# Chunk-selected attention with a gated convolution block: the selection masks of the later pairs transposed by DMA instead of TensorE

## The chip, the core and the metric

The kernel runs on one core of a Trainium2 chip. A core has five engines, each with its own queue of instructions that it works through in order: TensorE (PE; the loading of its weights is listed apart as PEld), VectorE (DVE), ScalarE (ACT), GpSimd (POOL) and SyncE (SP), which here does nothing but issue DMAs. Engines wait for each other by semaphores only. The metric is the device time of one execution in microseconds: 198.59 us before the change (median of 3 runs, 198.16 to 199.49). The profiled execution has a span of 195.8 us.

## The reference

There are 4 batches, 8 heads, 768 positions and a head dimension of 64, all in float32. The keys are cut into 24 chunks of 32. For each query, an upper bound of its score with each chunk is computed from the chunk's elementwise minimum and maximum; the 6 chunks with the highest bounds, among those that are not in the future, are kept, and ordinary causal attention runs on these alone:

```python
k_min = np.min(k_chunks, axis=3)
k_max = np.max(k_chunks, axis=3)
ub = np.sum(np.maximum(q[:, :, :, None, :] * k_min[:, :, None, :, :],
                       q[:, :, :, None, :] * k_max[:, :, None, :, :]), axis=-1)
ub = np.where(causal, ub, -1000000000.0)
top_chunks = np.argsort(ub, axis=-1)[..., -top_k:]
scores = scale * np.matmul(q, k.transpose(0, 1, 3, 2))
sel = (j_chunk == top_chunks[..., None]).any(axis=-2)
mask = sel & (pos[:, None] >= pos[None, :])
scores = np.where(mask, scores, -1000000000.0)
```

The attention output x, 768 x 512 per batch, then goes through a gated block: a causal convolution over 5 positions per channel gives the gate, `x @ w_val` the value, and the result is `(sigmoid(conv(x)) * (x @ w_val)) @ w_out`.

## The kernel before, in words

**Pairs.** Two heads of one batch make a pair; there are 16 pairs, numbered 0 to 15, four per batch. A pair passes through these stages:

- `load`: k, q and v of both heads come by DMA (192 KB for one head), three pairs ahead of their use.
- `kq`: TensorE transposes k and q in float32 (L561). ScalarE copies them out of PSUM (L576, L622, L634), VectorE takes the minima and maxima of chunks (L581), GpSimd writes the operands KE and QU of the score matmul in float16 (L606, L653).
- `sel` and `part`, the selection, on which the change bears. For each of the five blocks of 128 queries after the first, two float32 matmuls (L727) give the bounds of both heads. VectorE adds a term for the query's own chunks (L740), finds the sixth highest bound with ten MAX8 instructions (L746), and one comparison (L753) writes `NS`, a 128 x 5 x 128 tile that says for each query which chunks are not selected. The score matmul wants this with chunks on the partitions. So TensorE transposes the five blocks into a PSUM bank (L764), and two copies (L787) of 24 partitions x 640, one on VectorE for head 0 and one on ScalarE for head 1, bring the rows into `QU`.
- `attn`: the score matmuls (L860) contract over 64 rows of q and k and, in the same pass, over the 24 mask rows, against constant rows that are -240 where a key lies in that chunk: a chunk that isn't selected gets a large negative score. There are 28 such matmuls for a pair, in 11 PSUM banks. ScalarE takes the exponential of each bank (L867), GpSimd zeroes the future part of diagonal blocks (L874), 42 matmuls multiply by v (L891), VectorE divides by the sums (L817, L821), and a DMA transpose (`to_xT`, L833) puts the result in the layout that the gated block wants.
- `moe_gate`, `moe_val`, `moe_out`: the gate of a pair's 128 channels is one convolution tap on TensorE (L932), four on VectorE (L956) and a tanh on ScalarE (L961). After every fourth pair, a batch's values (L975), products (L982) and outputs (L991, L997) follow, and stores to HBM (L1004).

**The order of the work** is not written by hand. The code registers every operation with an engine, a cost, a key (a due time in units of pairs), what it reads and writes, and which buffers it takes. `Plan.order` then starts operations one after the other on a model of the engines: on each engine the one with the lowest key among those that could start about earliest. The table `SHIFT` moves the keys by kind of operation ("DVE:QM" for the mask copies on VectorE, "PE:s" for the scores; a leading 0 is for the first pair), and `CAPS` says how many of the eight PSUM banks each use may hold. The outcome is one list, and each engine's queue is its part of that list. DMAs are operations of SyncE. When one has been started, the model does this:

```python
            elif e in ("SP", "ACTQ"):
                free[e] = s + 0.55
                dma = max(dma, s + 1.6) + o.cost
                o.end = dma + 0.8
            ...
            for d in o.outs:
                if d.eng != e:
                    d.ready = max(d.ready, o.end)
                elif e != "PE":
                    d.ready = max(d.ready, free[e] + 0.06)
```

**Buffers.** QU and KE have three copies each, used in turn by pair, so mask rows of pair p can only be written when the scores of pair p - 3 are done. NS has two copies. A switch `MDMA` stood at 99, which no pair reaches; the branch that it guards was unused.

Of the kernel before, what the change touches and what calls it, by code (L numbers as in the profile page):

```python
# [10 lines left out]
F16 = mybir.dt.float16  # L11
# [293 lines left out]
def kernel(  # L305
# [10 lines left out]
    nc = tc.nc  # L316

    B, H, S, D = q.shape
# [12 lines left out]
    CP = (slice(64, 64 + NCH), slice(0, NCH))  # L331
# [4 lines left out]
    SEL0 = 128  # L336
    SELT = NT - 1
# [5 lines left out]
    X0 = XP - (KSZ - 1)  # L343
    MASKS = ("DVE", "ACT")

    MDMA = 99
    KBPOOL = True

    SHUF = 99
# [8 lines left out]


    SHIFT = {  # L360
        "0SP:kn": -1.6, "0SP:qn": -1.1, "0SP:cwn": 3.4, "0DVE:warmup": 3.35, "0POOL:E00": -5.1,
        "0POOL:cfill": -4.5, "0DVE:KB": 0.9, "0DVE:QM": 2.7, "0POOL:VA": -3.3, "PE:pcw": 1.4,
        "0DVE:kmx": -3.1, "0DVE:kmn": -2.3, "0ACT:KE": -1.9, "0DVE:kmrr": 1.1, "0PE:qnT": 1.4,
        "0ACT:rq": 2.5, "SP:qn": -1.3, "PE:pu": 2.5, "DVE:top8": 1.8, "PE:sT": 0.1,
        "DVE:QM": 1.8, "ACT:QM": -3.0, "PE:knT": -0.92, "ACT:k32": -1.3, "DVE:kmx": 1.0,
        "DVE:kmn": 1.5, "POOL:kmrr": -0.7, "POOL:KBh": -7.4, "PE:qnT": -0.87, "ACT:q32": -1.6,
        "ACT:rq": -1.1, "POOL:QU": 1.5, "POOL:VA": 1.2, "PE:s": 0.14, "bank0": 1.1, "ACT:P": 1.9,
        "POOL:Ptri": -1.6, "PE:av": -4.2, "bank1": 0.34, "bank2": -3.5, "0PE:av": 3.77,
        "DVE:rcp": 2.0, "DVE:onat": -4.0, "bank3": 1.0, "bank4": -0.6, "bank5": 1.3,
        "bank6": 0.5, "bank7": -1.9, "bank8": 0.2, "bank9": 0.72, "bank10": 0.9, "PE:pg": 2.1,  # L370
        "PE:pv": 2.66, "DVE:gv": -2.9, "PE:po": 2.5, "ACT:osb": 2.3,
    }
    CAPS = {"w": 5, "s": 4, "av": 2, "spare": 1, "v": 4}
    BUFS = {"kn": 3, "qn": 3, "vn": 3, "P5": 2, "kmx": 2, "kmr": 2,
# [14 lines left out]
    junk = cpool.tile([128, 512], F16, tag="junk")  # L389
    warmup = cpool.tile([128, 1], FP, tag="warmup")  # L390
    cfill = cpool.tile([128, SELT, 2, 4], FP, tag="cfill")
# [19 lines left out]
    T = {}  # L411
# [22 lines left out]
    def act(key, cost, fn, r=(), w=(), new=()):  # L434
        plan.add("ACT", key, cost, fn, r, w, new)
# [7 lines left out]
    def sp(key, kb, fn, r=(), w=(), new=(), eng="SP", rate=205.0, at=0.0):  # L443
        plan.add(eng, key, kb / rate, fn, r, w, new, at=at)
# [263 lines left out]
    def part(p, key, g, its, nch, kb, qu, ns, iN, i2):  # L708
        pu, n, i0 = ("pu", p, g), len(its), its[0] - 1
        i1 = i0 + n  # L710

        def cols(t):

            x = "p (s c) -> p s c" if len(t.shape) == 2 else "p i (s c) -> p i s c"
            y = t.rearrange(x, s=2)
            return y[:, :, 0:nch] if len(t.shape) == 2 else y[:, :, :, 0:nch]

        first = new(pu, "w", [128, n * (2 * NCH + 4) + 4 * its[0]])
        kbr = [("KBh", i2, hh, w) for hh in range(2) for w in range(nch // 12)]

        def bound(i):
            return T[pu][:, i * 2 * NCH:(i + 1) * 2 * NCH]

        for it in its:
            ts = slice(it * 128, (it + 1) * 128)
            for j, x in enumerate(("rq", "q32")):
                pe(key, 128, lambda it=it, ts=ts, j=j, x=x: nc.tensor.matmul(  # L727
                    out=cols(bound(it - 1 - i0)), lhsT=T[x, p][:, ts],
                    rhs=cols(kb[:, j, :]), start=(j == 0), stop=(j == 1)),
                    r=[(x, p), (x, p, it // 3)] + kbr,  # L730
                    w=((pu, it),), new=first if it == its[0] and j == 0 else (), kind="u")
                plan.also((pu,))

        def own():

            x, d = 2 * NCH + 4, 4 * its[0]
            t = T[pu][:, d:d + n * x].rearrange("p (i x) -> p i x", i=n)
            return t[:, :, 0:2 * NCH].rearrange("p i (s c) -> p i s c", s=2)[:, :, :, 0:4]

        dve(key, 0.12, lambda: nc.vector.tensor_tensor(  # L740
            out=own(), in0=own(), in1=cfill[:, i0:i1], op=ALU.add),
            r=[pu, "cfill"] + [(pu, it) for it in its], w=((pu, "own"),))
        for it in its:
            m = 4 * it + 4
            for s in range(2):
                dve(key + 0.1, 0.08, lambda it=it, s=s, m=m: nc.vector.max(  # L746
                    out=T["top8", p][:, it - 1, s, :],
                    in_=bound(it - 1 - i0)[:, s * NCH:s * NCH + m]),
                    r=(pu, (pu, it), (pu, "own")), w=(("top8", p, it, s),),
                    new=new(("top8", p), "top8", [128, SELT, 2, 8])  # L750
                    if it == 1 and s == 0 else ())
                plan.also((("top8", p),))
        dve(key + 0.2, 0.07 + n * nch * 2 / 960, lambda: nc.vector.tensor_tensor(  # L753
            out=ns.rearrange("p i (s c) -> p i s c", s=2)[:, i0:i1, :, 0:nch],
            in0=cols(T[pu][:, 0:n * 2 * NCH].rearrange("p (i c) -> p i c", i=n)),
            in1=T["top8", p][:, i0:i1, :, 5:6].to_broadcast([128, n, 2, nch]), op=ALU.is_lt),
            r=[pu, (pu, "own"), ("top8", p)] + [(pu, it) for it in its]
            + [("top8", p, it, s) for it in its for s in range(2)]
            + ([("NS", i2, 1 - g)] if len(its) < SELT else []),
            w=[("NS", i2, g)] if len(its) < SELT else [("NS", i2, 0), ("NS", i2, 1)])  # L760
        pt = ("sT", p, g)
        q0, nq = its[0] * 128, n * 128
        for i in range(n):
            pe(key + 0.3, 128, lambda i=i: nc.tensor.transpose(  # L764
                out=T[pt][:, i * 128:(i + 1) * 128], in_=ns[:, i0 + i, :], identity=identh),
                r=(("NS", i2, g), "identh"), w=((pt, i),),
                new=new(pt, "w", [128, nq], F16) if i == 0 else (), kind="x")
            plan.also((pt,))

        def mask(key, hh, fn, r, w):  # L770
            if MASKS[hh] == "ACT":
                act(key, 0.2 + nq * 0.0006, lambda: fn(copy=nc.scalar.copy), r, w)
            else:
                dve(key, 0.14 + nq * 0.00057, lambda: fn(copy=nc.vector.tensor_copy), r, w)

        ws = (g,) if len(its) < SELT else (0, 1)
        if p >= MDMA:
            act(key + 0.35, 0.14 + nq * 0.0007, lambda: nc.scalar.copy(out=T["m16", p], in_=T[pt]),
                r=[pt] + [(pt, i) for i in range(n)], w=(("m16", p),),
                new=new(("m16", p), "m16", [128, S - SEL0], F16))  # L780
            for hh in range(2):
                sp(key + 0.35, 60, lambda hh=hh: nc.sync.dma_start(
                    out=qu[CP[hh], hh, SEL0:S], in_=T["m16", p][CP[hh], :]),
                    r=(("m16", p),), w=[("QM", iN, hh, w) for w in ws])
            return
        for hh in range(2):
            mask(key + 0.35, hh, lambda hh=hh, copy=None: copy(  # L787
                out=qu[CP[hh], hh, q0:q0 + nq],
                in_=T[pt][CP[hh], :]),
                r=[pt] + [(pt, i) for i in range(n)], w=[("QM", iN, hh, w) for w in ws])  # L790
# [14 lines left out]
    def attn(p, key):  # L805
# [24 lines left out]
        def to_xT(ws, kk):  # L830
            t0, n = 3 * ws[0], 3 * len(ws)
            if p < NPAIR - 1:
                sp(kk, n * 32, lambda: nc.sync.dma_start_transpose(  # L833
                    out=xT[:, slot, XP + t0 * 128:XP + (t0 + n) * 128]
                    .rearrange("p (t r) -> p t r", t=n),
                    in_=T["onat", p][:, t0:t0 + n, :].rearrange("p t d -> p (t d)")),
                    r=[("onat", p)] + [("onat", p, w) for w in ws],
                    w=[("xT", slot, w) for w in ws], rate=200.0)
                return
            pt = ("xTp", p, ws[0])  # L840
            for i in range(n):
                pe(kk, 128, lambda i=i: nc.tensor.transpose(
                    out=T[pt][:, i * 128:(i + 1) * 128], in_=T["onat", p][:, t0 + i, :],
                    identity=identh),
                    r=(("onat", p), ("onat", p, (t0 + i) // 3), "identh", pt), w=((pt, i),),
                    new=new(pt, "w", [128, n * 128], F16) if i == 0 else (), kind="x")
            act(kk, 0.11 + n * 0.0915, lambda: nc.scalar.copy(
                out=xT[:, slot, XP + t0 * 128:XP + (t0 + n) * 128], in_=T[pt]),
                r=[pt] + [(pt, i) for i in range(n)], w=[("xT", slot, w) for w in ws])
# [266 lines left out]
```

## Time and profile before

| what | value |
|---|---|
| time, median of 3 runs | 198.59 us |
| span of the profiled execution | 195.8 us |
| DMA traffic | 29.56 MB, mean 151 GB/s |
| transposes of the masks, TensorE (L764) | 80 instructions |
| copies of the masks (L787) | 17 on ScalarE, 17 on VectorE |
| DMAs with transposes (L833) | 15, landing after a median of 3.6 us |

When a pair's mask was made and used (us from the start, read from the trace):

| pair | bounds done | NS done | first transpose | copies done (ACT, DVE) | first score |
|---|---|---|---|---|---|
| 8 | 80.8 | 89.3 | 89.4 | 90.7, 91.5 | 90.9 |
| 9 | 90.5 | 98.8 | 99.0 | 100.2, 102.1 | 100.6 |
| 11 | 111.0 | 114.9 | 116.0 | 117.2, 119.2 | 119.5 |
| 13 | 133.1 | 136.5 | 136.5 | 137.8, 140.2 | 140.2 |
| 15 | 152.9 | 155.3 | 156.2 | 157.3, 158.4 | 158.5 |

In the groups of the profile a line reads: source line, engine, operation, what is written and read, how many; then the sum of their busy times and the mean length of one in ns; then how long the engine had been idle just before them and what ended most of that. "SPq" is SyncE's queue. The chain of work that ended last is followed back from the last instruction, at each step to what released it. A TensorE record includes the time in the array, so neighbouring records overlap.

### The profile page before, as it was taken

The numbers are of one execution on the slowest core, as the hardware profiler recorded it, in microseconds if no ns is written. First come the engines' busy times: TensorE is split into PE (matmuls) and PEld (weight loads), VectorE is DVE, ScalarE is ACT, GpSimd is POOL, SyncE is SP. The second block draws the span as 40 slices with busy tenths as digits, with TensorE's granted clock in tenths as the row PEclk, the third lists the DMA queues.
The fourth block names the chain that finished last, engine by engine and source line by source line (L and its number), as shares of the span: only waits on it lengthen the run. The fifth ranks groups of instructions, "written<-read, shape, count | busy, mean of one in ns | idle before, by whom it ended". The sixth has DMA issues, their size and how long they took to land.

```text
span 195.8 us, 5815 instructions
## 1 busy us (share of the span) xinstructions
PE 181.2 (93%) x2043; PEld 144.2 (74%) x2043; DVE 177.5 (91%) x540; ACT 162.1 (83%) x355; POOL 122.9 (63%) x274
## 2 busy tenths in 40 slices
PE   6598989999589999999999999999999999999981
PEld 2377878989568988888887878797979657765530
DVE  7839599979889999899999999999999999999981
ACT  3688969999969999997979999998897999945431
POOL 8029779889767998889894856886788334200000
PEclk9889999999999999999999999999999999999999
DMA  6999999999999999997997664242005430305244
GB/s 135 223 217 216 211 223 180 151 229 212 188 228 221 190 179 181 183 177 163 146 181 180 172 148 139 87 90 44 2 5 147 122 136 7 75 3 216 111 162 161
DMA packets 91900, 29.56 MB, mean 151 GB/s; under 512 B 87754, under 2 KB 88798, under 8 KB 91870
## 3 DMA queue, kind: packets, MB, share of 16 engines
q1 hardware_dynamic: 89214, 27.74, 70.1%
q0 software_dynamic: 1056, 1.05, 3.8%
q10 hardware_dynamic: 1600, 0.39, 1.0%
q8 instruction: 16, 0.26, 0.6%
q14 instruction: 14, 0.11, 0.2%
HBM read 20.98 MB, written 6.29 MB: 139 GB/s over the span
## 4 chain that ended last, share of the span: by engine, by line
PE 63%; DVE 16%; ACT 9%; DMA 5%; issue 2%; POOL 2%; SPq 1%; ACTq 0%; POOLq 0%
PE banks L860 13%; PE banks L727 11%; PE banks L975 9%; PE banks L991 9%; PE banks L891 8%; PE banks L561 7%; DVE banks L956 6%; ACT t_P L867 5%; PE banks L932 4%; DMA t_kn<-in_k_dram 3%; DMA xT<-t_onat 2%; PE banks L764 2%; DVE t_kmx L581 2%; DVE t_kmr L581 1%; PE banks L543 1%
## 5 line engine op out<-in xcount | busy, mean ns | idle before, releaser
L867 ACT ACTIVATE t_P<-banks 128x512 f16<-128x512 f32 (+1 forms) x176 | 91.4, 599 | 4.4 <-PE banks L860 4.2
L956 DVE SCALAR_TENSOR_TENSOR banks<-xT,cwT,banks 128x384 f32<-128x384 f16 x128 | 77.1, 619 | 2.7 <-PE banks L932 1.9
L860 PE MATMUL banks<-QU,KE 128*128 128x128 f16 (+4 forms) x448 | 65.6, 246 | 1.6 <-DVE QU L787 0.7
L874 POOL TENSOR_SCALAR_AFFINE_SELECT t_P<-t_P 128x384 f16<-128x384 f16 x64 | 32.8, 522 | 24.9 <-ACT t_P L867 23.8
L860 PEld LDWEIGHTS <-KE 128*128 128x128 f16 (+1 forms) x448 | 39.3, 108 | 8.3 <-DVE QU L787 1.3
L606 POOL CAST KE<-t_k 64x384 f16<-64x384 f32 x60 | 30.0, 504 | 13.8 <-ACT t_k L576 9.4
L653 POOL CAST QU<-t_q 64x384 f16<-64x384 f32 x60 | 30.3, 504 | 3.1 <-ACT t_q L622 0.7
L891 PE MATMUL banks<-VA,t_P 128*128 128x65 f16 x672 | 29.8, 194 | 0.6 <-ACT t_rq L634 0.4
L891 PEld LDWEIGHTS <-t_P 128*128 128x128 f16 x672 | 26.3, 98 | 5.1 <-POOL t_P L874 1.4
L975 PE MATMUL banks<-xT,wval_sb 128*128 128x384 f16 x128 | 29.6, 325 | 0.1
L727 PE MATMUL banks<-KB,t_rq 128*128 128x48 f32 (+1 forms) x160 | 27.9, 256 | 0.0
L727 PE MATMUL banks<-KB,t_q 128*128 128x48 f32 (+1 forms) x160 | 27.6, 254 | 0.0
L727 PEld LDWEIGHTS banks<-KB,t_rq 128*128 128x128 f32 x160 | 26.1, 191 | 1.5 <-DVE t_onat L821 0.7
L727 PEld LDWEIGHTS banks<-KB,t_q 128*128 128x128 f32 x160 | 26.2, 191 | 0.3
L991 PE MATMUL banks<-wout_sb,t_gv 128*128 128x512 f16 x96 | 25.8, 379 | 0.6 <-DVE t_gv L982 0.6
L961 ACT ACTIVATE t_g<-banks 128x384 f32<-128x384 f32 x32 | 16.0, 500 | 5.8 <-DVE banks L956 5.7
L561 PE MATMUL banks<-ident,t_kn 128*128 128x128 f32 x96 | 17.3, 286 | 2.6 <-DMA t_kn<-in_k_dram 2.3
L932 PE MATMUL banks<-xT,diag 128*128 128x384 f16 x64 | 17.4, 326 | 2.3 <-DMA xT<-t_onat 2.0
L622 ACT ACTIVATE t_q<-banks 128x384 f32<-128x384 f32 x32 | 16.0, 501 | 3.7 <-PE banks L561 3.6
L576 ACT ACTIVATE t_k<-banks 128x384 f32<-128x384 f32 x32 | 16.3, 512 | 2.9 <-PE banks L561 2.6
L997 ACT ACTIVATE t_osb<-banks 128x512 f32<-128x512 f32 x22 | 13.2, 600 | 6.3 <-PE banks L991 4.2
L821 DVE TENSOR_TENSOR t_onat<-banks,t_rcp 128x384 f16<-128x384 f32 x32 | 17.7, 553 | 0.2
(62 smaller groups left out, 264.5 us busy)
## 6 DMA issues: line engine op xcount, KB each, us to landing
t_vn<-in_v_dram SPq DMA_DIRECT2D x32, 192.0 KB, 4.3
out_dram<-t_osb SPq DMA_DIRECT2D x24, 256.0 KB, 2.2
t_kn<-in_k_dram SPq DMA_DIRECT2D x30, 192.0 KB, 4.6
t_qn<-in_q_dram SPq DMA_DIRECT2D x30, 192.0 KB, 3.9
wval_sb<-in_moe_w_val_dram POOLq DMA_DIRECT2D x1, 512.0 KB, 7.3
wout_sb<-in_moe_w_out_dram POOLq DMA_DIRECT2D x1, 512.0 KB, 7.3
xT<-t_onat SPq DMA_TRANSPOSE x15, 3.6
t_kn<-in_k_dram ACTq DMA_DIRECT2D x2, 96.0 KB, 3.1
```

The source lines that it names most:

```text
L561: lambda tl=tl: nc.tensor.transpose(out=T[name][:, tl * 128:(tl + 1) * 128], in_=T[which, p][:, 3 * w + tl, :], identity=ident),
L606: pool(k0 + 0.6, 0.56, lambda hh=hh: nc.gpsimd.tensor_copy(out=ke[HP[hh], hh, sl], in_=T["k32", p][HP[hh], sl]), r=(("k32", p), ("k32", p, ...
L653: pool(k0 + 0.3, 0.56, lambda hh=hh: nc.gpsimd.tensor_copy(out=qu[HP[hh], hh, sl], in_=T["q32", p][HP[hh], sl]), r=(("q32", p, w), ("q32", ...
L727: pe(key, 128, lambda it=it, ts=ts, j=j, x=x: nc.tensor.matmul(out=cols(bound(it - 1 - i0)), lhsT=T[x, p][:, ts], rhs=cols(kb[:, j, :]), s ...
L860: pe(kk, m, lambda hh=hh, c=c, jt=jt, q0=q0, m=m, bank=bank: nc.tensor.matmul(out=T[bank][:, c:c + m], lhsT=ke[KP[hh], hh, jt * 128:(jt + ...
L867: nc.scalar.activation(out=T[pt][:, 0:width], in_=T[bank][:, 0:width], func=AF.Exp, scale=0.125),
L874: nc.gpsimd.affine_select(out=ap, in_=ap, pattern=[[0, tris], [1, 128]], compare_op=ALU.is_ge, fill=0.0, base=0, channel_multiplier=-1)
L891: nc.tensor.matmul(out=T[pav][:, o0:o0 + D + 1], lhsT=T[pt][:, col:col + 128], rhs=va[:, hh, jt, :], start=st, stop=sp_, skip_group_check= ...
L932: nc.tensor.matmul(out=T[pg], lhsT=diag[ct][:, ki, hl, :], rhs=xT[:, slot, X0 + w * HB + ki:X0 + w * HB + ki + HB], start=(n == 0), stop=( ...
L956: nc.vector.scalar_tensor_tensor(out=both() if whole else T[pgs[w]], in0=x_of(X0 + ki, w), scalar=cwT[:, i:i + 1], in1=both() if whole els ...
L975: lambda ct=ct: nc.tensor.matmul(out=T[pv], lhsT=wval_sb[:, ct, et * 128:(et + 1) * 128], rhs=xT[:, slot0 + ct, XP + w * HB:XP + (w + 1) * ...
L991: pe(key, DM, lambda et=et: nc.tensor.matmul(out=T[po], lhsT=T["gv", b, et][:, s * 128:(s + 1) * 128], rhs=wout_sb[:, et, :], start=(et == ...
```

## The change

From pair 8 on the mask takes another road. SyncE issues a DMA that transposes the whole `NS` tile (five blocks of 128 x 128) into a new SBUF tile `m16`, and two DMAs that copy 24 rows of 640 from `m16` into `QU`, one for each head. The TensorE transposes, the PSUM bank and the two copies of these pairs are gone. Pairs 0 to 7 keep the old road. The planner's rate for the DMA transposes of the attention output is set from 200 to 133. `SHIFT` has new values throughout, so the order of all operations is a different one, in the first half too.

```diff
-    MDMA = 99
+    MDMA = 8
...
     SHIFT = {
...
+        q0, nq = its[0] * 128, n * 128
+        if p >= MDMA:
+            sp(key + 0.3, 160, lambda: nc.sync.dma_start_transpose(
+                out=T["m16", p], in_=ns.rearrange("p i c -> p (i c)")),
+                r=(("NS", i2, 0), ("NS", i2, 1)), w=(("m16", p),),
+                new=new(("m16", p), "m16", [128, SELT, 128], F16), rate=133.0)
+            for hh in range(2):
+                sp(key + 0.35, 60, lambda hh=hh: nc.sync.dma_start(
+                    out=qu[CP[hh], hh, 128:S],
+                    in_=T["m16", p][CP[hh]].rearrange("p i c -> p (i c)")),
+                    r=(("m16", p),), w=[("QM", iN, hh, w) for w in range(2)], rate=240.0)
+            return
         pt = ("sT", p, g)
-        q0, nq = its[0] * 128, n * 128
...
         ws = (g,) if len(its) < SELT else (0, 1)
-        if p >= MDMA:
...
-            return
...
-                    w=[("xT", slot, w) for w in ws], rate=200.0)
+                    w=[("xT", slot, w) for w in ws], rate=133.0)
```

## The prediction, made before the result was known

> **What bounds the kernel now.** I read the busy line of the page first, then busy time by stretch from pair 8 on, then TensorE's waits, then the groups that the change removes, then the DMA landings.
>
> ```profile
> PE 181.2 (93%) x2043; PEld 144.2 (74%) x2043; DVE 177.5 (91%) x540; ACT 162.1 (83%) x355; POOL 122.9 (63%) x274
> ...
> PE 63%; DVE 16%; ACT 9%; DMA 5%; issue 2%; POOL 2%; SPq 1%; ACTq 0%; POOLq 0%
> ```
>
> Three engines are nearly full, and the chain that ended last runs mostly through TensorE. Busy time overstates them: records overlap. In the timeline a 128-column score starts 0.056 us after the one before it, though its record is 0.219 us long; a VectorE multiply-add (L956) starts 0.525 us after its neighbour with a record of 0.62. So I count spacings: 0.030 us for a P·V matmul, 0.163 for 384 columns, 0.216 for 512, 0.16 for a bound matmul (L727), 0.109 for a float32 transpose.
>
> ```profile
> 90.00:160.00 70.00, 69.94 (x821) 57.22 (x820) 68.77 (x210) 64.00 (x138) 50.14 (x110) 1.00 0.51 117
> 160.00:172.00 12.00, 11.85 (x182) 8.70 (x178) 12.00 (x28) 11.00 (x24) 3.63 (x7) 1.00 0.24 57
> 172.00:196.00 24.00, 18.98 (x104) 9.23 (x101) 18.48 (x36) 9.44 (x18) 0.00 (x0) 0.99 0.36 132
> ```
>
> Columns: length, then busy time of PE, PEld, DVE, ACT, POOL, then clock, DMA share and GB/s. From 90 to 160 us, where masks 9 to 15 are made, TensorE's spacings sum to 67.3 of 70.0 us; those of VectorE to about 93%, of ScalarE to about 86%. TensorE is the bound, with only 2.7 us of small waits left; VectorE is next. DMA is half idle there, and nearly so after 130 us.
>
> ```profile
> PE banks L764 <- DVE NS L753: 1.3, 2, 0.9
> PE banks L860 <- DVE QU L787: 0.7, 1, 0.7
> ```
>
> These are all of TensorE's long waits for a mask (total, times, longest), and both lie before 30 us. From pair 8 on a mask is never waited for long: its road is short.
>
> **What the Trainium skill says.** "DMA: Bandwidth & Descriptors", Rules for kernel authors: a DMA that reads what an earlier DMA wrote must wait for that one's completion semaphore before it is issued; the same queue doesn't order them. The same page, Anatomy of one DMA: the wait happens on the issuing sequencer, and a fixed part, about 2 us for DMAs issued from GpSimd, is mostly the wait for the last write's receipt. The trace agrees on the size: stores of 256 KB land 2.0 us after issue when nothing else runs. It shows no DMA that waits for another's data. "Perfetto Trace Analysis", Optimizing Scalar/DVE Operations: instruction latency exceeds engine time, since the write acknowledgement overlaps the next instruction. The trace agrees: 0.62 against 0.525 us above.
>
> **What goes.** For eight pairs:
>
> ```profile
> L787 ACT COPY QU<-banks 24x640 f16<-24x640 f16 (+2 forms) x17 | 11.1, 652 | 2.3 <-PE banks L764 2.2
> L787 DVE COPY QU<-banks 24x640 f16<-24x640 f16 (+2 forms) x17 | 8.0, 469 | 1.1 <-ACT QU L787 0.6
> L764 PE MATMUL banks<-identh,NS 128*128 128x128 f16 x80 | 7.6, 220 | 1.3 <-DVE NS L753 1.3
> ```
>
> TensorE: 8 x 5 transposes x 0.056 = 2.24 us, all of it on the bounding engine. VectorE: 8 x 0.52 (spacing of the 640-wide copy) = 4.2 us. ScalarE: 8 x 0.58 = 4.6 us. These two are not the bound; what they bring is fewer of the 2.7 us of waits, and a bank less in use per pair. In the tail, 24 us hold 18.8 us of TensorE spacings and VectorE is full from 172 to 184, so a lighter VectorE can shorten it: I take 1 us (bounds 0 and 2). I cost the memory and DMA traffic at nothing: eight transposes of 160 KB and sixteen small copies go into queues half idle from 100 us on.
>
> **What comes: a longer road.** All DMAs go through SyncE. Its chain is now: wait for NS, issue the transpose, wait until it has landed, issue copy 0, issue copy 1; TensorE's first score of each head waits for its copy.
>
> ```profile
> L833 SPq DMA_TRANSPOSE xT<-t_onat x15: 1212/1222/2605, 30.8 to 169.2; - x15
> ...
> DMA to landing us min/median/max: 2.8/3.6/4.7
> ```
>
> The nearest row, a transpose of six blocks against five here, lands after 2.8 us when the queue is empty (all those after 130 us) and 4.4 when loads are ahead (92 us). The copy of 24 rows of 1280 B is shown nowhere; I bound it by 1.6 and 2.3 us empty (the smallest store landing is 2.0), and take 1.9; under loads 2.7, the least landing of a load near there, with 3.5 as the upper bound. With 0.1 us between, the mask of head 0 comes 2.8 + 0.1 + 1.9 = 4.8 us after the issue (bounds 4.3 and 5.3), under loads 4.4 + 0.1 + 2.7 = 7.2 (5.6 to 8.0). Head 1 follows 0.4 later, more if other issues stand between.
>
> Is that much work ahead of the score in TensorE's order? The order of the changed kernel tells. I counted the matmuls between the transpose and the first score of head 0 and 1, in the single list that the planner writes out, and priced them with the spacings times 70.0/67.3. First a test on the kernel before, from the start of NS to the first score: counted 1.8, 2.0, 2.5, 5.0, 1.8, 3.9, 2.6, 3.6 us for pairs 8 to 15; the trace has 2.0, 2.2, 2.8, 5.0, 1.8, 4.1, 2.5, 3.6. The count is good to 0.3 us. For the changed kernel, head 0/head 1: pair 8 6.5/6.8, pair 9 4.2/4.6, pair 10 7.7/7.8, pair 11 6.0/6.3, pair 12 5.4/5.7, pair 13 4.1/5.4, pair 14 4.1/6.7, pair 15 4.3/5.3. Pair 9, for one: 35 matmuls, of them 11 x 0.056 + 12 x 0.109 + 4 x 0.163 + 4 x 0.16 + 4 x 0.216 = 4.1, x 1.04 = 4.2.
>
> Why four pairs stand so close to 4.1: in `order`, an operation that follows another on the same queue is ready at free[e] + 0.06, and SyncE is free 0.55 us after an issue. So the planner lets the copies go 0.6 us after the transpose is issued, not when it has landed, and puts the scores too near.
>
> TensorE then stalls, since its order is fixed: pair 8 (loads) 7.2 - 6.5 = 0.7; pair 9 (loads) 7.2 - 4.2 = 3.0; pairs 10 to 12 nothing; pair 13 4.8 - 4.1 = 0.7, and 0.3 for head 1, whose copy is queued behind an output transpose of 1.2 us; pair 14 0.7; pair 15 0.5. Sum 5.9 us. With the lower bounds 1.4 + 0.2 + 0.2 = 1.8; with the upper ones 1.5 + 3.8 + 1.5 + 1.2 + 1.0 = 9.0.
>
> What is queued behind SyncE's wait: loads of pairs 12 to 15, output transposes, stores. None is urgent: between an output transpose's issue and the gate matmul that reads it the new order has 8 to 10 us for most pairs, and 3.9 for pair 14, past the last mask.
>
> **Sum.** Stalls partly take the place of the small waits, because the banks are drained while TensorE stands. Waits in the stretch go from 2.7 (3.1 over the eight pairs) to 5.9 + 0.5 = 6.4: +3.3. Work: -2.24. Tail: -1. Net +0.1 us: 198.7. The new order keys also rearrange pairs 0 to 7; there TensorE loses some 8 us between 20 and 60 us to small waits and one of 2.0 us for an output transpose at 54 us, whose booked rate is now more cautious (133 instead of 200). I can't price that; +-1.5 us.
>
> **Rivals.** (1) Faster: the transposes land early and the lower bounds hold: waits 1.8 + 0.5 against 3.1, so -0.8 - 2.24 - 1 = -4.0, 194.6 us. For it: DMA is idle late, three engines get lighter. Against it: the slack of 4.1 us is less than even 4.3. (2) Slower: upper bounds, with nothing won in the tail: 9.0 + 0.5 - 3.1 - 2.24 = +4.2, 202.8 us. For it: loads ahead of masks 8 and 9, SyncE's wait, which delays its other issues. Against it: after 110 us few loads are left. (3) VectorE is the true bound, and TensorE's stalls cost nothing while VectorE has work: then the gain is VectorE's 4.2 us less the part idle in the stalls, about 196. VectorE's 93% speaks against it.
>
> **How the numbers follow.** No change within 1% (196.6 to 200.6), 0.37: likeliest, as gains of 3 to 4 us and stalls of 2 to 9 us are of one size. Faster by over 1% (rivals 1 and 3), 0.34. Slower by over 1% (rival 2), 0.29. The range: 194.9, near rival 1, to 202.4, near rival 2.
>
> **What would show it.** 40 transposes and 8 copies on each engine gone. TensorE's waits list a DMA of the mask copies with 2 to 9 us, the longest at pair 9, then 13 to 15, none at 10 to 12; SyncE waits about 3 us per pair for its own transpose. Wrong if no such waits appear (the copy lands faster than 1.6 us, or NS comes earlier), if they appear at every pair, or if the early pairs move by more than 2 us.

## The result, and the profile after

The changed kernel takes 210.17 us (median of 4 runs, 209.31 to 210.97) against 198.38 us of the kernel before on the same chip: a ratio of 1.059, 95% interval 1.051 to 1.067. It is slower by 5.9%, well above the range of the prediction. The span of its profiled execution is 207.6 us, 11.8 us more than before. A median here or below is of all runs, while a ratio is meant to leave out executions in a slower state of the chip, so the two can differ by half a per cent.

The busy line and the chain of the page after:

```profile
PE 182.7 (88%) x2003; PEld 144.3 (70%) x2003; DVE 173.9 (84%) x532; ACT 158.9 (77%) x347; POOL 122.0 (59%) x274
...
PE 50%; DMA 17%; DVE 13%; ACT 11%; issue 3%; SPq 2%; POOL 1%; ACTq 0%; DVEq 0%; POOLq 0%
```

The work has gone as planned: 40 TensorE instructions less, 8 copies less on each of two engines. Yet every engine is busy for a smaller share of the span, and DMA, 5% of the chain before, is now 17% of it. TensorE's waits (total, times, longest):

```profile
PE banks L862 <- DMA QU<-t_m: 9.9, 12, 2.3
PE banks L560 <- DMA t_kn<-in_k_dram: 3.9, 3, 1.5
```

The first row says that the scores (L862 now) wait for the mask copies. The same stretches as before, by time, to the last P·V matmul and from there to the end (length, busy time of PE, PEld, DVE, ACT, POOL, clock, DMA share, GB/s):

```profile
90.00:185.00 95.00, 83.59 (x983) 65.36 (x982) 78.76 (x232) 74.16 (x161) 54.49 (x120) 0.98 0.53 116
185.00:208.00 23.00, 17.74 (x109) 8.89 (x104) 17.31 (x35) 9.09 (x18) 0.00 (x0) 0.94 0.37 138
```

Priced with the spacings, TensorE's time without work is 22.5 us at 90 us, against 22.0 before: the first half is unchanged within 0.5 us. From there to the last P·V matmul it grows by 17.9 us, where before it grew by 4.2. After that it is 5.1 against 5.3. So 13.7 us of new time without work in the second half, less 2.2 us of removed work, plus 0.5 early, make the 12 us. These are estimates from the spacings; the 13.7 also holds some 1.7 us in which TensorE worked at half clock (last section).

Where they fall, from the trace (us; the stall is the gap before the first score of each head less the usual 0.11, both heads added):

| pair | NS done | transpose issued | first copy issued | first score | stall | predicted |
|---|---|---|---|---|---|---|
| 8 | 88.6 | 90.5 | 94.2 | 96.5 | 1.4 | 0.7 |
| 9 | 101.5 | 101.5 | 105.1 | 107.1 | 2.1 | 3.0 |
| 10 | 111.6 | 114.8 | 118.5 | 120.6 | 2.0 | 0 |
| 11 | 121.7 | 126.0 | 129.3 | 131.4 | 2.4 | 0 |
| 12 | 139.5 | 139.6 | 142.2 | 145.1 | 0 | 0 |
| 13 | 147.0 | 147.0 | 149.6 | 151.7 | 1.5 | 1.0 |
| 14 | 159.1 | 159.2 | 161.9 | 164.0 | 1.3 | 0.7 |
| 15 | 165.1 | 166.6 | 171.1 | 173.2 | 3.0 | 0.5 |

The sum is 13.7 us; that it equals the growth above is chance, since the growth also holds the slower clock and somewhat fewer small waits. Look at the third column: the masks of pairs 8, 10, 11 and 15 are ready 1.5 to 4.2 us before SyncE issues their transpose. SyncE's waits for mask transposes in the whole run (total, times, longest), and its queue around pairs 10 and 11, in the trace (start, length; L763 is the mask transpose, L768 its copies):

```profile
SPq L768 <- DMA t_m<-NS: 14.7, 7, 3.1
...
110.44 0.54 SPq L462 DMA_DIRECT2D t_vn<-in_v_dram  x1
111.08 0.81 SPq L1006 DMA_DIRECT2D out_dram<-t_osb  x1
111.93 0.43 SPq L462 DMA_DIRECT2D t_kn<-in_k_dram  x1
112.46 2.22 SPq L1006 DMA_DIRECT2D out_dram<-t_osb  x1
114.78 1.23 SPq L763 DMA_TRANSPOSE t_m<-NS  x1
118.50 1.55 SPq L768 DMA_DIRECT2D QU<-t_m  x2
120.15 0.46 SPq L1006 DMA_DIRECT2D out_dram<-t_osb  x1
120.70 1.35 SPq L835 DMA_TRANSPOSE xT<-t_onat  x1
122.15 1.11 SPq L462 DMA_DIRECT2D t_qn<-in_q_dram  x2
123.36 0.49 SPq L1006 DMA_DIRECT2D out_dram<-t_osb  x1
123.90 1.11 SPq L462 DMA_DIRECT2D t_vn<-in_v_dram  x2
125.11 0.75 SPq L1006 DMA_DIRECT2D out_dram<-t_osb  x1
125.95 1.28 SPq L763 DMA_TRANSPOSE t_m<-NS  x1
```

There is one gap, 116.0 to 118.5: the wait for its own transpose. Everything else is back to back. From 86 to 133 us, SyncE's issues take 34.4 us of 47 (19.9 before), and the four gaps between a transpose and its first copy another 9.1. Little is left over; mask 11's transpose waits behind stores and loads which were themselves held up by mask 10. Issues of one kind differ in length (the stores above take 0.46 to 2.22 us); why some are long isn't shown.

### The profile page after: what moved, and what is told of

Its sections match the earlier page's. It is cut to its first block, busy times and chain, and to the rows that moved or that the text cites. A ratio compares the mean times of both kernels' runs of the same rounds, so it can differ in the third digit from the quotient of the medians.

```text
span 207.6 us, 5757 instructions
## 1 busy us (share of the span) xinstructions
PE 182.7 (88%) x2003; PEld 144.3 (70%) x2003; DVE 173.9 (84%) x532; ACT 158.9 (77%) x347; POOL 122.0 (59%) x274
## 4 chain that ended last, share of the span: by engine, by line
PE 50%; DMA 17%; DVE 13%; ACT 11%; issue 3%; SPq 2%; POOL 1%; ACTq 0%; DVEq 0%; POOLq 0%
PE banks L726 9%; PE banks L862 9%; PE banks L993 7%; DVE banks L958 6%; PE banks L977 6%; PE banks L893 6%; DMA t_kn<-in_k_dram 6%; DMA QU<-t_m 6%; PE banks L560 6%; DMA t_m<-NS 5%; ACT t_P L869 5%; PE banks L934 3%; ACT t_q L621 2%; PE banks L542 2%; ACT t_rq L633 2%
## 5 line engine op out<-in xcount | busy, mean ns | idle before, releaser
L869 ACT ACTIVATE t_P<-banks 128x512 f16<-128x512 f32 (+1 forms) x176 | 93.0, 602 | 21.0 <-PE banks L862 17.2
L862 PE MATMUL banks<-QU,KE 88*128 88x128 f16 (+5 forms) x448 | 64.9, 247 | 12.0 <-DMA QU<-t_m 9.9
L862 PEld LDWEIGHTS <-KE 88*128 88x128 f16 (+1 forms) x448 | 38.3, 107 | 19.5 <-DMA QU<-t_m 11.2
L893 PEld LDWEIGHTS <-t_P 128*128 128x128 f16 x672 | 27.0, 100 | 5.3 <-POOL t_P L876 1.4
L993 PE MATMUL banks<-wout_sb,t_gv 128*128 128x512 f16 x96 | 27.2, 379 | 0.0
L726 PEld LDWEIGHTS banks<-KB,t_q 128*128 128x128 f32 x160 | 26.8, 191 | 0.6
L726 PE MATMUL banks<-KB,t_q 128*128 128x48 f32 (+1 forms) x160 | 27.1, 251 | 0.0
L984 DVE SCALAR_TENSOR_TENSOR t_gv<-t_g,banks 128x384 f16<-128x384 f32 x32 | 17.3, 549 | 5.3 <-PE banks L977 5.2
L580 DVE TENSOR_REDUCE t_kmx<-t_k 128x12 f32<-128x384 f32 x32 | 16.9, 542 | 3.9 <-ACT t_k L575 3.8
L575 ACT ACTIVATE t_k<-banks 128x384 f32<-128x384 f32 x32 | 15.7, 497 | 4.1 <-POOL KE L605 1.4
```

The source lines that it names most:

```text
L862: pe(kk, m, lambda hh=hh, c=c, jt=jt, q0=q0, m=m, bank=bank: nc.tensor.matmul(out=T[bank][:, c:c + m], lhsT=ke[KP[hh], hh, jt * 128:(jt + ...
L869: nc.scalar.activation(out=T[pt][:, 0:width], in_=T[bank][:, 0:width], func=AF.Exp, scale=0.125),
L893: nc.tensor.matmul(out=T[pav][:, o0:o0 + D + 1], lhsT=T[pt][:, col:col + 128], rhs=va[:, hh, jt, :], start=st, stop=sp_, skip_group_check= ...
L993: pe(key, DM, lambda et=et: nc.tensor.matmul(out=T[po], lhsT=T["gv", b, et][:, s * 128:(s + 1) * 128], rhs=wout_sb[:, et, :], start=(et == ...
```

## Experiments

Theory A is that the scores' waits for the road make the loss. B puts it on the new keys, C on the transposes' own traffic and issue time, D on SyncE standing still whether or not a score waits. Later letters are explained where they are used.

**The order keys alone, and the road alone.**

```diff
# keys alone: the changed kernel with
-    MDMA = 8
+    MDMA = 99
# road alone: the changed kernel with SHIFT and the rate of 200 of the kernel before
```

> The changed kernel with its order keys, but all masks on the old road (TensorE transposes and two copies). Theory A, the loss is TensorE waiting for the masks of pairs 8 to 15: the waits go, 196 to 201 us. Rival B, the new order of all operations is itself slow (the early stall for k at 47 us, the half clock after it): 204 us or more.

> The kernel before, its own order keys and its rate of 200, with the DMA road for masks 8 to 15. Theory A: slower than before by 4 to 8 percent, 206 to 214 us, with 10 us or more of TensorE waits for the mask copies. Rival B: within 2 percent of before.

The keys alone: 199.86 us, ratio 1.012 (1.009 to 1.016). The road alone: 209.18 us, 1.055 (1.046 to 1.064), with 8.1 us of waits on the TensorE row for the mask copies, less than the 10 expected. The new order is about 1% slower by itself; the rest is the road, whatever the keys. Rival B fell, and by these times theory A held.

**No road: the copies left out, then the transposes too.**

```diff
-                sp(key + 0.35, 60, lambda hh=hh: nc.sync.dma_start(
-                    out=qu[CP[hh], hh, 128:S], ...),
+                sp(key + 0.35, 60, lambda: None,
# and in the second run
-            sp(key + 0.3, 160, lambda: nc.sync.dma_start_transpose(...),
+            sp(key + 0.3, 160, lambda: None,
```

> The changed kernel in the same order, its two mask copies per pair left out for pairs 8 to 15, so that their scores take the rows that lie in QU from before; the transposes are still issued, but nothing waits for them. Theory A: TensorE's 13.7 us of stalls and the half clock at 175 us (1.7 us) go, 194 to 198 us. Rival C, the transposes' DMA traffic and issue time slow the rest: 202 us or more.

> As the run before it, with the eight mask transposes left out as well: no road at all for masks 8 to 15. Theory A: within 1 us of the run that keeps the transposes. Rival C: faster than that by 3 us or more.

Without copies: 195.15 us, ratio 0.984 (0.978 to 0.991). Without transposes as well: 196.39 us, 0.989 (0.983 to 0.995). The intervals overlap, though the medians lie 1.2 us apart, a little more than the 1 us expected. In the traces that difference lies ahead of the road: NS of pair 8 is done at 87.8 and at 89.1 us, and from there to the end both runs take 105.3. So the transposes' traffic and issue time cost nothing that can be measured (rival C fell). The copies and what waits for them cost 210.17 - 195.15 = 15.0 us (on two chips, where the kernel before takes 198.38 and 198.49), and the removed work, with no copies in its place, is worth 199.86 - 195.15 = 4.7 us (the planner's order differs between these two as well).

**SyncE waits, the scores don't.** The copies run, but into a tile that nobody reads.

```diff
+    scr = cpool.tile([128, 2, S - 128], F16, tag="scr")
...
-                    out=qu[CP[hh], hh, 128:S],
+                    out=scr[CP[hh], hh, :],
```

> The changed kernel in the same order; transposes and copies run as in it, with SyncE's wait between them, but the copies land in a tile that nobody reads, and the scores of pairs 8 to 15 take the rows that lie in QU from before. Theory A, only the scores' waits cost: 194 to 198 us. Rival D, SyncE standing still for about 3 us per pair delays loads, output transposes and stores enough to cost time by itself: 200 us or more.

204.58 us, ratio 1.028 (1.022 to 1.035). This was the surprise. No score waits for a mask, yet by the medians 9.4 of the 15.0 us remain. TensorE's waits say where:

```profile
PE banks L935 <- DMA xT<-t_onat: 5.6, 2, 3.1
PE banks L561 <- DMA t_kn<-in_k_dram: 4.3, 2, 2.8
```

The first row wasn't there before with any weight from 60 us on: at 138 and 175 us, gate matmuls now wait for the output transposes, which SyncE issues late. The second row isn't the road's: its longest wait, 2.8 us, ends at 48.5 us, before any mask takes the road, and its length changes from run to run. So a comparison of whole runs may overstate the case. Counted in the traces from NS of pair 8 to the end, this run takes 113.0 us, the run without copies 105.3 and the changed kernel 119.0: 7.7 of 13.7 us remain. Theory A, that only the scores' wait costs, fell; rival D, that SyncE standing still costs by itself, held. The exact share isn't shown, since SyncE waits longer for its transposes here (18.4 us in the whole run against 14.7).

**The stores out of SyncE's queue.**

```diff
-        sp(key, 256, lambda: nc.sync.dma_start(out=out[b, ...
+        sp(key, 256, lambda: nc.scalar.dma_start(out=out[b, ...
```

> The changed kernel in the same order, with the 24 stores issued from ScalarE's queue, right behind the copy that fills them, instead of SyncE's. Theory A2, a large part of the stalls is that SyncE comes late to the transpose (1.9, 3.2, 4.2, 1.5 us after NS for pairs 8, 10, 11, 15) because it is full of other issues: masks 10 to 15 come earlier, 204 to 208 us. Rival E, the road of transpose and copy by itself makes the stalls: 209 to 211 us.

209.40 us, ratio 1.053 (1.048 to 1.058), against 1.059 for the changed kernel: no difference beyond the intervals, where A2 expected 204 to 208 us. Taking 24 short issues away leaves the 9 us of waiting for the transposes where it was. It does bring masks forward: the transposes of pairs 10, 11 and 15 are issued 1.7, 3.0 and 0.0 us after NS instead of 3.2, 4.2 and 1.5. But the wait for mask 10 grew (3.6 us, with its first copy 4.3 us on its way to the score instead of 2.1), and from 98.9 to 129.6 us TensorE was at half clock for 10.2 us; the changed kernel has 3.4 us of that, at 174.6 us. So A2 fell by its time (rival E's 209 to 211 us held), and whether a shorter SyncE queue is worth anything by itself isn't told by this run, which also puts the stores' issue on ScalarE.

**The copies four issues later in SyncE's queue, nothing else moved.**

```diff
+    held, queue, given = [], [], 0
+    for o in order:
+        if held and (given >= 4 or set(o.reads + o.writes) & {x for h in held for x in h.writes}):
+            queue += held
+            held, given = [], 0
+        if getattr(o, "grp", "") == "SP:QM" and o.reads[0][1] < 12:
+            held.append(o)
+            continue
+        given += 1 if held and o.eng == "SP" else 0
+        queue.append(o)
+    order = queue + held
```

> The changed kernel, every other queue as in it; only in SyncE's queue the two copies of masks 8 to 11 stand four issues later, so that loads, output transposes and stores go out while the transpose is under way. Theory D, SyncE is full from 86 to 133 us (34 us of issuing and 9 us of waiting in 47) and so comes late to everything: 5 to 8 us better than the changed kernel, 202 to 206 us, the stalls of pairs 10 and 11 mostly gone. Rival A, the scores stand too near the mask and SyncE's queue doesn't matter: 208 us or more.

219.48 us, ratio 1.104 (1.094 to 1.114). Theory D, as put here, fell; rival A's "208 us or more" held, but neither expected it to be so much worse.

```profile
PE banks L862 <- DMA QU<-t_m: 17.1, 9, 4.8
```

SyncE's gaps before the copies of masks 8 to 11 went (from 9.1 us in all to the 0.1 us between any two issues), and the transposes of masks 10 and 11 are issued 0.0 and 1.4 us after NS instead of 3.2 and 4.2. But the copies are issued 5.1 to 6.6 us after their transpose instead of 3.4 to 3.7, and the score that waits for them starts 2.8 to 4.0 us after their issue instead of 2.0 to 2.2, perhaps because of the loads that now go first (not tested); the stall at pair 8 is 5.2 us. From 97 us on, during and after the long stalls, TensorE is also at half clock for 13.6 us in all (3.4 in the changed kernel, from 90 us to the last P·V matmul). Filling SyncE's wait didn't help while the scores stayed where they were.

**From pair 12 on only.**

```diff
-    MDMA = 8
+    MDMA = 12
```

> The changed kernel with the DMA road from pair 12 on only, when no load is left. Theory A: the stalls of four masks remain, 5 to 8 us with the half clock, less half of the 4.7 us that the removed work is worth: 202 to 206 us. Rival F, only SyncE's load issues make the masks late, so that late pairs gain: below 199 us.

204.26 us, ratio 1.028 (1.018 to 1.038). The four runs are far apart, from 201.34 to 206.41 us, and the two fastest lie only 2.0 and 3.6 us above the kernel before on that chip (199.31), of which the new keys' 1.2% explains most. So the size of this loss is uncertain. That the road stalls TensorE without any load in SyncE's queue is shown by the trace of the fastest run, where the last load is issued at 124 us and the first mask transpose at 133:

```profile
PE banks L862 <- DMA QU<-t_m: 4.2, 6, 2.0
```

The rival that only the loads in SyncE's queue make the road dear (F) fell: no run came near the 199 us or less that it expected.

**The planner's belief mended.** One condition: on SyncE, too, an operation is ready when the one that it follows has landed.

```diff
-                if d.eng != e:
+                if d.eng != e or e == "SP":
                     d.ready = max(d.ready, o.end)
```

> The changed kernel with one condition altered in the planner: an operation on SyncE that follows another one is ready when that one has landed, as for other engines. Same keys. The other issues then fill SyncE's wait, and the scores stand further behind the mask. Theory A, the planner's belief put the scores too near: most stalls go, 197 to 204 us. Rival E, a road of 6 us or more doesn't fit into this pipeline wherever the scores stand: 207 us or more.

197.78 us, ratio 0.995 (0.992 to 0.998): 12.4 us better than the changed kernel, with the same keys, the same instructions and the same DMAs in another order. TensorE's waits for masks in the trace:

```profile
PE banks L862 <- DMA QU<-t_m: 1.0, 1, 1.0
```

In the new order 8 to 12 us lie between a mask's transpose and the first score that reads it in every pair from 8 to 15 but three (11, 12, 13, at 6.5 to 7.2), and SyncE never stands still for a transpose: each copy follows the issue before it within 0.12 us. The road has not become shorter; it lies beside other work. Two things that looked like causes are still there: SyncE's issues take 39.1 us of the 47 from 86 to 133, more than in the changed kernel, and the transposes of pairs 10 and 11 are issued 2.6 and 4.5 us after NS. So neither a full queue nor a late transpose cost much by itself here; what cost was SyncE standing still, and scores that stood nearer than the road is long.

**The same mend with the old keys, and with new ones.**

> The kernel before with its own keys and rate, the DMA road from pair 8 on, and the planner's readiness mended as in the run that did so with the new keys. If the planner's belief is the cause whatever the keys: 195 to 201 us, against 209.2 with the same keys and the belief unmended. If the new keys were needed for the mend to work: 203 us or more.

> The kernel before's keys, the DMA road from pair 8 on and the readiness mended, once more, on the same chip as the run with new keys: 195.5 to 198 us, 1 to 1.5 percent faster than before.

Both are the same kernel, with the old keys, on two chips: 196.91 us, ratio 0.987 (0.984 to 0.991), and 196.66 us, 0.990 (0.987 to 0.993), against 209.18 with the same keys and the belief unmended. The mend works with either set of keys. In the next run the planner also gets the measured lengths of SyncE's issues, and new keys:

```diff
-                free[e] = s + 0.55
-                dma = max(dma, s + 1.6) + o.cost
+                free[e] = s + {"SP:m16": 1.25, "SP:xT": 1.25, "SP:QM": 0.82,
+                               "SP:out": 0.45}.get(o.grp, 0.55)
+                dma = max(dma, s + (1.1 if o.grp == "SP:QM" else 1.6)) + o.cost
# and other values in SHIFT
```

> The DMA road from pair 8 on with the planner mended: an operation on SyncE that follows another waits for its landing, and SyncE is held for the measured times (1.25 us for a transpose, 0.82 for a mask copy, 0.45 for a store). The order keys are new, searched for this planner. If the road pays once the order knows its length: faster than the kernel before and than the mended planner with the old keys (196.9 us), 192 to 196 us. If the removed work brings nothing more than those: 196 to 199 us.

192.35 us, ratio 0.973 (0.968 to 0.978): faster than both kernels. Its busy line:

```profile
PE 178.2 (93%) x2008; PEld 143.0 (75%) x2008; DVE 170.9 (90%) x532; ACT 157.3 (83%) x347; POOL 121.8 (64%) x274
```

How much of this last step is due to the road's better fit and how much to keys that would help the old road as well stays open: new keys without the road weren't run.

## Why the prediction was wrong, step by step

**What goes: right in kind, a little low.** The sum put the removed work at 2.24 us, 1 us in the tail and part of the small waits. With no copies in its place it measured 4.7 us.

**The planner's readiness as the cause: right.** The prediction named the condition, and mending that line alone gave 12.4 us back.

**The length of the road: right on an empty queue, too long under loads.** It was put at 4.8 us on an empty queue. For pairs 13 and 14 the trace has 4.7 and 4.8 (146.97 to 151.70, 159.16 to 163.99). Under loads it was put at 7.2; pairs 8 to 11 show 5.5 to 6.0. The copies' landing, shown nowhere before, is 2.0 to 2.2 us by the score that waits for it; 1.9 and 2.7 were taken. Head 1 follows 0.8 to 1.0 us later, not 0.4, because the issue of one such copy takes SyncE 0.77 us. (The bounds of 4.3 and 5.3 us don't follow from the terms given: 2.8 + 0.1 with 1.6 and 2.3 are 4.5 and 5.2. The sums change by little.)

**The failed step: "None is urgent."** The prediction looked at what stands behind SyncE's wait and asked only whether those transfers are urgent. It put SyncE's standing still at nothing and didn't add up SyncE's time. Issuing rises from 19.9 to 34.4 us of 47 and 9.1 us of waiting come on top, so little is left over, and the next mask's transpose is itself one of the transfers behind the wait. This is why "pairs 10 to 12 nothing" failed: pairs 10 and 11 stall 4.4 us together, with a transpose 3.2 and 4.2 us late. The slacks of 7.7 and 6.0 us had been counted from the transpose's place in the order, as if it were issued when NS was done. Pair 15 has the same fault (0.5 predicted, 3.0 measured): its transpose is 1.5 us late and lands after 4.4 us behind two stores. The run with copies into an unread tile shows the fault by itself: 7.7 of the 13.7 us that the road costs from pair 8 on, with no score waiting for a mask, through output transposes for which the prediction saw "8 to 10 us" of room. The rest goes with the scores, which wait for masks whose transposes come late; the two can't be added up exactly.

**"Stalls partly take the place of the small waits": too hopeful.** The sum had 6.4 us of waits in all; the stretch shows 17.9. The stalls' 13.7 and the clock's 1.7 leave about 2.5 us of small waits, where 4.2 stood before and 0.5 were counted on. So 2 us at most were absorbed.

**A cost left out: the clock.** A long stall was in some cases followed by a stretch of TensorE at half clock (1.7 us in the changed kernel). The chances were spread over three cases, and the slower rival ended at 202.8; with SyncE's fullness left out, even its upper bounds were too low.

## What to carry to other kernels

Putting work on an issuing queue adds its waits as well as its issues: before moving a chain of dependent DMAs there, add up issue time and wait time per period and compare with the period, and count the next transfer of the same kind among those that stand behind the wait. If the sum is tight, put other issues into the wait. The chain of two dependent DMAs took 4.7 to 6.6 us here; it cost little when both the consumer's order and the issuing queue's order left that room, and moving SyncE's copies alone made things worse. When a hand-made scheduler decides the order, read what it believes of a dependence inside one queue before trusting the slack that it leaves.

## What the runs showed of the hardware

TensorE's granted clock fell to half for 3.4 us after the longest stall (2.7 us, ended at 173.2 us), by the windows of the changed kernel (clock before the last two columns):

```profile
170.00:174.00 4.00, 1.66 (x22) 0.99 (x20) 2.12 (x5) 1.79 (x4) 1.04 (x2) 1.00 0.24 79
174.00:179.00 5.00, 4.79 (x41) 3.12 (x38) 2.56 (x6) 2.91 (x7) 0.52 (x1) 0.66 0.21 41
```

From 174.6 to 178.0 us it is 0.5, which costs another 1.7 us of work; the mask stalls of 2.0 us and less in the same run left it at 1.0. (Half clock also shows from 48.3 to 51.7 us, after TensorE's waits for loads of K, before any mask takes the road.) The length of one stall doesn't decide it. With the road alone, gaps of 1.8 and 2.1 us (ended at 108.8 and 118.7 us) were each followed by 3.4 us at half clock; with copies into an unread tile a gap of 2.5 us (138.1) was, and one of 3.1 us (175.0) wasn't. What decides isn't shown. The stretches at half clock that begin and end within the profiled work lasted 3.4 or 6.8 us in every trace here.

A DMA copy of 24 rows holds SyncE for 0.77 us (median of 16 in the changed kernel, 0.71 to 0.88), a copy of 128 partitions for 0.33 to 0.37 where it was shortest.
